# Scores paired by halves, one burst of probability-times-v products a unit, and three score banks a pass, in an adaLN block with segmented attention and a SwiGLU feed-forward

## The chip, the cores and the metric

The kernel runs on one core of a Trainium2 chip. The metric is the device time of one execution in microseconds (us). Before the change three executions took 1886.43, 1879.5 and 1883.25 us, with a median of 1883.25 us.

Engines: PE is the matrix engine (TensorE), PEld its loading of weights, DVE VectorE, ACT ScalarE, POOL GpSimd, and SP the engine that issues most DMAs. PE writes only into PSUM, which has 8 banks of 128 partitions x 512 fp32 numbers; DVE and ACT read the banks.

## The reference, cut to what matters

```python
h = layernorm(x) * (1 + ca) + sa                 # x: 2048 x 576; 32 heads of 18; 4 segments of 512
for s in range(4):                               # per segment and head
    logits = qs @ ks.T * scale + mask            # 512 x 512, causal
    a_dot = softmax(logits) @ vs
    a_mem = phi(qs) @ M / (phi(qs) @ z + 1e-6)   # M, z: from the segments before
    o = g * a_mem + (1 - g) * a_dot
    M += phi(ks).T @ vs;  z += phi(ks).sum()
x = x + ga * (o @ wo)
h = layernorm(x) * (1 + cb) + sb
x = x + gb * ((silu(h @ w_gate) * (h @ w_up)) @ w_down)
```

## The kernel before

There are three stages. Until 237 us, q, k and v are projected (`proj`, `vproj`) and stored in DRAM, for four segments of 512 tokens. From 237 to 592 us runs attention, with the products by `wo` of earlier segments and the preparation of the feed-forward's input mixed in. From 613 us to the end (a short rest of the `wo` products lies between) comes the feed-forward, whose code is the same in both kernels.

Attention works in 32 **units**, of one segment and four heads each (`units`, u = 8 s + q). A head has 18 features, and fp32 accuracy is had by stacking high and low parts, so a score product contracts over 54 or 56 rows. Heads with an even number lie in partitions 0 to 63 of the stacks `kst` and `qst` (half a), odd ones in 64 to 127 (half b). Two score products in different halves of the array can run at once. A score product thus uses PE as two tiles of 64 x 128. A product of exponentials and v uses it as four tiles of 128 x 32, one for each head; all others (`pw`, `px`, `pn`, `pto`, `pt`) use the full 128 x 128.

Each unit has two passes. **Pass 1** (`p1_step`, two units ahead) computes scores to find the row maximum: PE writes them into a bank of tag `s1` (L187), DVE takes the maximum (L206), and `mt_a`/`mt_b` (events m and n) transpose the maxima and put them by DMA into two rows of `qst` for each half. **Pass 2** (`p2_step`) computes the transposed scores less the maximum into a bank `s2` (L639), ACT takes the exponential into a tile `Pt` (L645), and POOL zeroes what the mask forbids (L649). `av_step` multiplies `Pt` with v into the bank `av` (L662) for key blocks j = 0 to 3 of 512, 384, 256 and 128 columns; `ev_step` (E) copies it out by ACT; `comb_a` and `comb_b` (c, d) transpose it back and scale it. `wo_m` and `wo_x` (M0 to M3, X) make a product with `wo` in the bank `pw`, `num_a` to `num_e` (A, B, C, D, G) are the part of the memory, and `trans4` and its successors (at steps from `KP`) prepare the feed-forward.

The order is written by hand. Every unit has eleven steps, and `PAT` (a row for each kind of unit: first or second half of a segment, even or odd) says which events each step issues, in this order on all engines. An event "a" is one call of `scores`: one bank's worth of pass 2 of unit u and one of pass 1 of unit u + 2, 12 calls in a unit. The engines run in order, each its own queue.

PSUM banks before: two `s1`, two `s2`, two `x` (for `px`, `pmt`, `pn`, `pto`, `ptr`, `pt` in turn), one `w` (for `pw`) and one `av`. While `w` has no other work (u < 11) every third bank of pass 1 is the `w` bank, and in units 0 to 3 every third of pass 2 is an `x` bank.

The first two units' pass 1 runs earlier, among the projections of segment 1 (`early`, `p1_unit`). It uses full-height products against `qe`, a copy of q in which the other half is zero.

Of the kernel before, what the change touches and what calls it, by code (L numbers as in the profile page):

```python
# [7 lines left out]
F32 = mybir.dt.float32  # L8
F32R = mybir.dt.float32r
# [6 lines left out]
P = 128  # L16
S = 2048
D = 576
# [4 lines left out]
L = 512  # L23
# [33 lines left out]
NE = 2  # L57
WQ = (0, 3, 4, 5, 6)
E1 = 3
E2 = 2  # L60
PAT = (("a", "a", "M0 a a", "V2 V3 m E D n", "a a", "M1 G c", "Q a a", "V0 M2 d", "a a", "h A0 q M3 R S P X T f a Y B0", "a Z A1 V1 z B1 C"),
# [3 lines left out]
LNA = 1  # L65
S1B, S2B, XB, WB = 2, 2, 2, 1


def f32(ap):
    return ap.bitcast(F32)  # L70
# [3 lines left out]
def block(ctx: ExitStack, tc: tile.TileContext, x, wqk, wv, wo, beta, wgu, wd, c, w_mod, wm01, out):  # L74
    nc = tc.nc
# [81 lines left out]
    turn = [0, 0]  # L157
    HS0 = [[[0, 1, 2, 3]], [[0, 1], [2, 3]]] + [[[0], [1], [2], [3]]] * 2
    HS1 = [[[1], [0], [3], [2]], [[1, 3], [0, 2]]]
    HS2 = [[[0], [1], [2], [3]], [[0, 2], [1, 3]]]  # L160

    def load_stack(u, b):
        s, q = units[u]
        for e in range(2):
            v = [d[s].rearrange("f z t -> (f z) t").rearrange("(Q a e r) t -> Q e r a t", Q=8, a=2, e=2)[q, e]
                 for d in (kD, qD)]
            r = slice(64 * e, 64 * e + 54)
            nc.sync.dma_start(f32(kst[b][r]), v[0])
            nc.sync.dma_start(f32(qst[b][r]), v[1])
            if u < NE:  # L170
                nc.sync.dma_start(f32(qe[u][r, e:4:2, :]), v[1])
# [6 lines left out]
    def p1_step(u, b, i, ps, jp, jb, spare=0, mms=None):  # L178
        if i == 3:
            mcol[u] = (mwk.tile([P, 4, 4], F32, tag="mx", name="mx"),  # L180
                       mwk.tile([P, 2, 2, 2, 4], F32R, tag="mc", name="mc"))
        mx, mc = mcol[u]
        n = 128 * (i + 1)

        def mm(bank, h, o):
            r = slice(64 * (h % 2), 64 * (h % 2) + 54)
            nc.tensor.matmul(bank[:, n * o:n * o + n], lhsT=qst[b][r, h // 2, 128 * i:128 * i + 128],  # L187
                             rhs=kst[b][r, h // 2, 0:n], start=True, stop=True)
        hss = HS1[n <= 256] if mms is not None else HS0[i]
        for hs in hss:  # L190
            turn[0] += 1
            if spare and turn[0] % 3 == 0:
                bank = ps.tile([P, L], F32, tag="w", name="s1", bufs=spare)
            else:
                bank = ps.tile([P, L], F32, tag="s1", name="s1", bufs=S1B)
            if mms is None:
                for o, h in enumerate(hs):
                    nc.tensor.matmul(bank[:, n * o:n * o + n], lhsT=qe[u][0:118, h, 128 * i:128 * i + 128],
                                     rhs=kst[b][0:118, h // 2, 0:n], start=True, stop=True)
            else:  # L200
                for o, h in enumerate(hs):
                    mms.append(lambda h=h, o=o, bank=bank: mm(bank, h, o))
                yield
            for o, h in enumerate(hs):
                junk = jp.tile([P, L], BF16, tag="junk", name="junk", bufs=jb)
                nc.vector.tensor_tensor_reduce(junk[:, :n], bank[:, n * o:n * o + n], tri[:, L - n:],  # L206
                                               1.0, -3e38, op0=ALU.add, op1=ALU.max, accum_out=mx[:, h, i:i + 1])
            if hs is not hss[-1]:
                yield
        if i == 0:  # L210
            mv = mx.rearrange("p (a e) i -> p e a i", e=2)
            nc.gpsimd.tensor_scalar(mc[:, :, 0], mv, -1.0, 0.0, op0=ALU.mult, op1=ALU.add)
# [12 lines left out]
        nc.scalar.copy(mr, pmt.pop(u)[:32, :P])  # L225
        put_m(u, u % NB)

    def p1_unit(u, b, ps, tag, bufs, jp, jb):
        for i in range(4):
            yield from p1_step(u, b, 3 - i, ps, jp, jb)  # L230
        for i in range(6 - 3 * u):
            yield
        mt_a(u, ps, tag, bufs)
        mt_b(u)
# [31 lines left out]
    with ExitStack() as p1:  # L266
# [6 lines left out]
        ps = pool(p1, "ps1", 2, space=PSUM)  # L273

        def early():
            q_ = pb.tile([P, 4, L], F32R, tag="qe", name="qe", bufs=1)
            nc.gpsimd.memset(f32(q_), 0.0)
            qe[0] = qe[1] = q_
            for u in range(NE):
                load_stack(u, u)  # L280
                yield from p1_unit(u, u, ps, "m", 1, pb, 2)
            load_stack(2, 2)

        wqkh = wq1.tile([P, 9, 5, P], F32R, tag="wqkh", name="wqkh")
# [328 lines left out]
    def load_unit(u):  # L613
        if u < NU:
            load_stack(u, u % NB)

    def p1_seq(u, mms):
        if NE <= u < NU:
            for i in range(4):
                yield from p1_step(u, u % NB, 3 - i, ps, wk, 4, WB if u < 11 else 0, mms)  # L620

    Pt, av = {}, {}

    def p2_step(u, j, mms):
        if u >= NU:
            return
        n = L - 128 * j
        pt = pp_.tile([P, 4, n], F32, tag=f"P{j}", name="Pt", bufs=1)
        Pt[u, j] = pt
        for hs in HS2[n <= 256]:  # L630
            turn[1] += 1
            if u < 4 and turn[1] % 3 == 0:
                bank = ps.tile([P, L], F32, tag="x", name="s2", bufs=XB)
            else:
                bank = ps.tile([P, L], F32, tag="s2", name="s2", bufs=S2B)
            for o, g in enumerate(hs):
                def mm(o=o, g=g, bank=bank):
                    r = slice(64 * (g % 2), 64 * (g % 2) + 56)
                    nc.tensor.matmul(bank[:, n * o:n * o + n],  # L639
                                     lhsT=kst[u % NB][r, g // 2, 128 * j:128 * j + 128],  # L640
                                     rhs=qst[u % NB][r, g // 2, 128 * j:L], start=True, stop=True)
                mms.append(mm)
            yield
            per = len(hs)
            nc.scalar.activation(pt[:, hs[0]:hs[-1] + 1:2, :n], bank[:, :n * per].rearrange("p (a b) -> p a b", a=per),  # L645
                                 AF.Exp, scale=SCALE)
            if hs is not HS2[n <= 256][-1]:
                yield
        nc.gpsimd.affine_select(out=pt[:, :, :P], in_=pt[:, :, :P], pattern=[[0, 4], [1, P]], compare_op=ALU.is_ge,  # L649
                                fill=0.0, base=0, channel_multiplier=-1)  # L650
        yield

    def av_step(u, j):
        if u < 0 or u >= NU:
            return
        s, q = units[u]
        if j == 0:
            av[u] = ps.tile([P, L], F32, tag="av", name="av", bufs=1)
        pt = Pt.pop((u, j))
        for h in range(4):  # L660
            hh = 4 * q + h
            nc.tensor.matmul(av[u][32 * h:32 * h + 32, 128 * j:L], lhsT=vq[s][:, j, VW * hh:VW * hh + 32],  # L662
                             rhs=pt[:, h, :L - 128 * j], start=(j == 0), stop=(j == 3))
# [92 lines left out]

    wps = {}

    def wo_m(s, i, h, c, wb=WB):
# [620 lines left out]
    def scores(ga, gb, ma, mb):  # L1380
        next(ga, None)
        next(gb, None)
        while ma or mb:
            for m in (ma, mb):
                if m:
                    m.pop(0)()
        next(ga, None)
        next(gb, None)

    with tc.manual_schedule():  # L1390
        new_stack(3, sk2)
# [56 lines left out]
        for i in range(4):  # L1448
            for h in range(2):
                for c in range(WC):  # L1450
                    n = 8 * i + 4 * h + c
                    wo_m(3, i, h, c, 2)
                    if c == 3:
                        wo_x(3, i, h)
                    flush()
# [232 lines left out]
```

## Time and profile before

| what | us |
|---|---|
| median of three executions | 1883.25 |
| the profiled execution | 1878.65 |
| its span, first to last instruction | 1876.9 |
| attention, first score product to last `px` product | 237.8 to 591.3 |
| PE / DVE / ACT / POOL busy over the span | 1846.5 / 1493.8 / 961.4 / 490.9 |

Busy PE time says little: a matmul is pipelined, the record of one lasts longer than the distance to the next, and a PE that starts its next matmul late still looks busy. What a matmul really costs is read from the distance between the starts of neighbours. An idle time of PEld (weight load) that ended on another engine is a wait that PE's busy time can hide. DVE and ACT records have hardly any overlap, so their busy time is their work.

### The profile page before, as it was taken

How to read it: one execution, taken by the hardware profiler on the slowest of the kernel's cores; microseconds unless marked ns; L12 is line 12 of the kernel's file. 1: busy time of each engine (PE TensorE's matmuls, PEld its weight loads, DVE VectorE, ACT ScalarE, POOL GpSimd, SP SyncE). 2: the span in 40 equal slices, each digit the busy share in tenths (PEclk: the TensorE clock that was granted, in tenths of full speed). 3: DMA queues.
4: the chain of work that ended last, by engine and by line, in shares of the span. 5: the costliest groups of instructions: out<-in, count | busy, mean ns of one | idle time of the engine just before them, and what ended most of it. 6: DMA issues, size and time to landing. Idle time of an engine off the chain costs nothing.

```text
span 1876.9 us, 30994 instructions
## 1 busy us (share of the span) xinstructions
PE 1846.5 (98%) x11061; PEld 1519.5 (81%) x11061; DVE 1493.8 (80%) x3309; ACT 961.4 (51%) x2137; POOL 490.9 (26%) x686
## 2 busy tenths in 40 slices
PE   8999999999999999999999999999999999999999
PEld 5888855666656888888888888888888888888888
DVE  7566378888885888888888889758888888888886
ACT  6344467667776544444544544434454454544442
POOL 2010036454565154454544454300000000000000
PEclk9999999999999999999999999999999999999999
DMA  8677655457655755455545534486333432333331
GB/s 299 220 230 264 230 158 152 139 144 198 172 157 179 272 171 192 164 167 196 176 163 167 163 125 155 149 279 188 107 100 99 126 103 88 114 104 125 103 101 51
DMA packets 177518, 304.49 MB, mean 162 GB/s; under 512 B 25156, under 2 KB 107012, under 8 KB 175444
## 3 DMA queue, kind: packets, MB, share of 16 engines
q1 hardware_dynamic: 149988, 248.66, 42.6%
q10 hardware_dynamic: 27376, 53.86, 8.1%
q8 instruction: 87, 1.43, 0.3%
q14 instruction: 67, 0.55, 0.1%
HBM read 188.42 MB, written 113.33 MB: 161 GB/s over the span
## 4 chain that ended last, share of the span: by engine, by line
PE 89%; DVE 4%; DMA 4%; ACT 2%; issue 1%; POOL 1%; SPq 0%; ACTq 0%; DVEq 0%
PE A L1227 23%; PE pd L1355 13%; PE C L1227 12%; PE pd L1336 10%; PE B L1227 6%; PE pp L100 5%; PE s L639 5%; PE av L662 4%; PE pw L771 3%; PE pv L100 3%; PE s L187 2%; DMA y<-yD 1%; PE pn L828 1%; PE px L683 1%; ACT Pt L645 1%
## 5 line engine op out<-in xcount | busy, mean ns | idle before, releaser
L1227 PE MATMUL A<-y,wh 128*128 128x512 f32 x1152 | 406.1, 393 | 2.0 <-DMA y<-yD 1.0
L206 DVE CUSTOM_DVE_ANT_0 junk<-s,tri 128x256 bf16<-128x256 f32 (+3 forms) x512 | 224.7, 486 | 61.8 <-PE s L187 52.5
L1227 PEld LDWEIGHTS A<-y,wh 128*128 128x128 f32 x1152 | 216.6, 188 | 46.9 <-ACT B L1273 2.2
L1192 DVE TENSOR_TENSOR wl<-O,wh 128x256 fp32r<-128x256 f32 x504 | 245.3, 492 | 2.1 <-ACT wh L1191 1.6
L1227 PE MATMUL A<-y,wl 128*128 128x512 f32 x576 | 226.8, 394 | 0.0
L645 ACT ACTIVATE Pt<-s 128x512 f32<-128x512 f32 (+2 forms) x384 | 183.1, 525 | 79.9 <-PE s L187 61.3
L1341 DVE TENSOR_TENSOR acc<-acc,pd 128x576 f32<-128x576 f32 x216 | 162.2, 751 | 59.0 <-PE pd L1336 51.6
L1227 PE MATMUL C<-y,wh 128*128 128x512 f32 x576 | 203.0, 393 | 0.5 <-DVE cu L1250 0.5
L1191 ACT CAST wh<-O 128x256 fp32r<-128x256 f32 x504 | 197.5, 405 | 1.2 <-DMA yD<-st 1.2
L1365 DVE TENSOR_TENSOR acc<-acc,pd 128x576 f32<-128x576 f32 x156 | 116.9, 750 | 92.2 <-PE pd L1355 91.4
L1355 PE MATMUL pd<-dh,ah 128*128 128x288 f32 x640 | 189.1, 295 | 0.5 <-DVE x L1359 0.5
L1355 PE MATMUL pd<-dh,al 128*128 128x288 f32 x640 | 189.1, 295 | 0.0
L1355 PE MATMUL pd<-dl,ah 128*128 128x288 f32 x640 | 188.8, 295 | 0.0
L1182 POOL TENSOR_TENSOR O<-O 128x384 f32<-128x384 f32 x132 | 149.7, 1147 | 147.3 <-DMA O<-in_wgu_dram 38.3
L1296 ACT CAST ah<-sg 128x512 fp32r<-128x512 f32 x192 | 119.2, 621 | 77.6 <-DVE sg L1251 71.4
L639 PE MATMUL s<-qs,ks 56*128 56x256 f32 (+3 forms) x512 | 141.0, 365 | 6.2 <-ACT Pt L645 5.5
L187 PE MATMUL s<-ks,qs 54*128 54x512 f32 (+1 forms) x480 | 138.9, 374 | 3.8 <-DMA qs<-qD 1.8
L1297 DVE TENSOR_TENSOR al<-sg,ah 128x512 fp32r<-128x512 f32 x192 | 133.6, 696 | 10.7 <-ACT ah L1296 10.5
L1336 PE MATMUL pd<-dh,ah 128*128 128x288 f32 x448 | 133.0, 297 | 0.0
L1336 PE MATMUL pd<-dh,al 128*128 128x288 f32 x448 | 132.5, 296 | 0.0
L1336 PE MATMUL pd<-dl,ah 128*128 128x288 f32 x448 | 132.3, 295 | 0.0
L649 POOL TENSOR_SCALAR_AFFINE_SELECT Pt<-Pt 128x512 f32<-128x512 f32 x128 | 81.5, 637 | 183.5 <-ACT Pt L645 182.9
(372 smaller groups left out, 4382.7 us busy)
## 6 DMA issues: line engine op xcount, KB each, us to landing
O<-in_wgu_dram SPq DMA_DIRECT2D x36, 768.0 KB
O<-oD SPq DMA_DIRECT2D x36, 512.0 KB
oD<-O ACTq DMA_DIRECT2D x34, 512.0 KB
ks<-kD SPq DMA_DIRECT2D x64, 216.0 KB
qs<-qD SPq DMA_DIRECT2D x64, 216.0 KB
O<-in_wgu_dram SPq DMA_DIRECT2D x36, 384.0 KB
rD<-wr ACTq DMA_DIRECT2D x36, 336.0 KB
wr<-rD SPq DMA_DIRECT2D x35, 336.0 KB
```

Of the source, the lines that this page charges most:

```text
L100: nc.tensor.matmul(ps, lhsT=a, rhs=b, start=(k == 0), stop=(k == 13))
L187: nc.tensor.matmul(bank[:, n * o:n * o + n], lhsT=qst[b][r, h // 2, 128 * i:128 * i + 128], rhs=kst[b][r, h // 2, 0:n], start=True, stop=True)
L206: nc.vector.tensor_tensor_reduce(junk[:, :n], bank[:, n * o:n * o + n], tri[:, L - n:], 1.0, -3e38, op0=ALU.add, op1=ALU.max, accum_out=mx ...
L639: nc.tensor.matmul(bank[:, n * o:n * o + n], lhsT=kst[u % NB][r, g // 2, 128 * j:128 * j + 128], rhs=qst[u % NB][r, g // 2, 128 * j:L], st ...
L645: nc.scalar.activation(pt[:, hs[0]:hs[-1] + 1:2, :n], bank[:, :n * per].rearrange("p (a b) -> p a b", a=per), AF.Exp, scale=SCALE)
L1182: eng.tensor_tensor(o[:, d], o[:, a], o[:, b], op=op)
L1191: nc.scalar.copy(wh, o)
L1192: later.append(lambda: nc.vector.tensor_tensor(wl, o, f32(wh), op=ALU.subtract))
L1227: nc.tensor.matmul(bank, lhsT=a, rhs=b, start=(first and n == 0), stop=(n == 6), skip_group_check=not first)
L1336: nc.tensor.matmul(pd[:, i, :288], lhsT=a[:, tk], rhs=w, start=(k == 0), stop=(k == 2))
L1341: nc.vector.tensor_tensor(o, o, pd[:, :, :288], op=ALU.add)
L1355: nc.tensor.matmul(pd[:, i, :288], lhsT=a[:, tk], rhs=w, start=(k == 0), stop=(k == 5))
```

## The change

Five things change, all before 613 us.

1. In `scores` the two lists of matmuls of a call are taken by their half, a first. The calls issue the pairs (a, b), (a, b) where they had issued (a, b), (b, a).
2. The four products of a unit with v stand together in one event, V0123, in the unit after (before: V0 and V1 in the unit itself, V2 and V3 in the one after). `Pt` has two buffers for each j instead of one.
3. Banks: three `s1`, three `s2`, two `x`. `av` and `pw` have no bank of their own any more, and take `x` banks in turn with the others. The spare banks of the first units are gone.
4. `PAT` and `KP` are other tables.
5. The stack of unit 3 is loaded ahead of v at the start of attention. In `early`, `qe` is three tiles of two heads instead of one of four, each unit's pass 1 goes by pairs of heads, and the q stacks of units 0 and 1 are loaded after `early` instead of in it.

```diff
-KP = (7, 8, 1, 3)
+KP = (10, 8, 10, 8)
...
-       ("a a Q", "l M0 a a", "D", "V2 V3 m n M1 E A0 a a", "", "G p M2 B0 a", "a", "M3 X A1 q c x d a a", "f", "B1 V0 C", "V1 Y h a P a"),
+       ("a Q", "a l V0123 E m a n", "", "a a M0 M1", "M2 a a p", "D", "x a a M3 X", "", "q a c a a", "Y P f", "d G"),
...
-S1B, S2B, XB, WB = 2, 2, 2, 1
+S1B, S2B, XB = 3, 3, 2
+PB = (2, 2, 2, 2)
...
-            turn[0] += 1
-            if spare and turn[0] % 3 == 0:
-                bank = ps.tile([P, L], F32, tag="w", name="s1", bufs=spare)
-            else:
-                bank = ps.tile([P, L], F32, tag="s1", name="s1", bufs=S1B)
...
+            bank = ps.tile([P, L], F32, tag="s1", name="s1", bufs=S1B if a is None else 2)
+            for o, h in enumerate(hs):
+                if a is None:
+                    mms.append((h % 2, lambda h=h, o=o, bank=bank: mm(bank, h, o)))
+                else:
+                    nc.tensor.matmul(bank[:, n * o:n * o + n], lhsT=qe[u, a][0:118, h % 2, 128 * i:128 * i + 128],
+                                     rhs=kst[b][0:118, a, 0:n], start=True, stop=True)
...
-            q_ = pb.tile([P, 4, L], F32R, tag="qe", name="qe", bufs=1)
-            nc.gpsimd.memset(f32(q_), 0.0)
-            qe[0] = qe[1] = q_
+            q_ = []
+            for n in range(3):
+                q_.append(pb.tile([P, 2, L], F32R, tag=f"qe{n}", name="qe", bufs=1))
+                nc.gpsimd.memset(f32(q_[n]), 0.0)
...
-        pt = pp_.tile([P, 4, n], F32, tag=f"P{j}", name="Pt", bufs=1)
+        pt = pp_.tile([P, 4, n], F32, tag=f"P{j}", name="Pt", bufs=PB[j])
...
-            turn[1] += 1
-            if u < 4 and turn[1] % 3 == 0:
-                bank = ps.tile([P, L], F32, tag="x", name="s2", bufs=XB)
-            else:
-                bank = ps.tile([P, L], F32, tag="s2", name="s2", bufs=S2B)
+            bank = ps.tile([P, L], F32, tag="s2", name="s2", bufs=S2B)
...
-            av[u] = ps.tile([P, L], F32, tag="av", name="av", bufs=1)
+            av[u] = ps.tile([P, L], F32, tag="x", name="av", bufs=XB)
...
-            wps[0] = ps.tile([P, L], F32, tag="w", name="pw", bufs=wb)
+            wps[0] = ps.tile([P, L], F32, tag="x" if s < 3 else "w", name="pw", bufs=XB if s < 3 else 2)
...
-            j = int(a)
-            av_step(u if j < 2 else u - 1, j)
+            for j in a:
+                av_step(u - 1, int(j))
...
-            for m in (ma, mb):
-                if m:
-                    m.pop(0)()
+            for m in sorted((m for m in (ma, mb) if m), key=lambda m: m[0][0]):
+                m.pop(0)[1]()
...
         new_stack(3, sk2)
+        load_unit(3)
         for j in range(4):
             load_v(0, j)
...
-            load_unit(u + 3)
+            if u:
+                load_unit(u + 3)
```

How the order moves is seen at three places. In the rows, `s` is a score bank of either pass (L639 before and L649 now: pass 2; L187 and L185: pass 1), and numbers at a name's end are buffers.

PE at the start of unit 11 (an odd unit, first half of its segment). Before, from its first score to its first `pw` products:

```order
L639 MATMUL s_4563<-qs_2718,ks_2719 128x512
L187 MATMUL s_4566<-ks_984,qs_983 128x512
L639 MATMUL s_4572<-qs_2718,ks_2719 128x512
L187 MATMUL s_4573<-ks_984,qs_983 128x512
L771 MATMUL pw<-woh,oh 128x288
L771 MATMUL pw<-wol,oh 128x288
L771 MATMUL pw<-woh,ol 128x288
L639 MATMUL s_4590<-qs_2718,ks_2719 128x512
L187 MATMUL s_4591<-ks_984,qs_983 128x512
L639 MATMUL s_4597<-qs_2718,ks_2719 128x512
L187 MATMUL s_4598<-ks_984,qs_983 128x512
L662 MATMUL av<-Pt,vq_3394 32x256 x4
```

Now, from the same score:

```order
L649 MATMUL s_4564<-qs_2728,ks_2729 128x512
L185 MATMUL s_4567<-ks_984,qs_983 128x512
L185 MATMUL s_4574<-ks_984,qs_983 128x512
L649 MATMUL s_4573<-qs_2728,ks_2729 128x512
L672 MATMUL av<-Pt,vq_3423 32x512 x4
L672 MATMUL av<-Pt,vq_3423 32x384 x4
L672 MATMUL av<-Pt,vq_3423 32x256 x4
L672 MATMUL av<-Pt,vq_3423 32x128 x4
L215 MATMUL pmt<-ident,mc 32x128
L649 MATMUL s_4608<-qs_2728,ks_2729 128x512
L185 MATMUL s_4609<-ks_984,qs_983 128x512
```

The four products with v (of unit 10) follow each other, scores stand on both sides of them, and the `pw` products come later in one row of ten. Within a group of four scores, pass 1 comes first in the second pair. Counted over the whole order from the first score of pass 2 to the last `px`, PE changes its tiling 391 times before and 251 times now: score bursts fall from 175 to 124, bursts of products with v from 88 to 32, the others from 153 to 123. Neighbouring scores of the same half fall from 206 to 8. The number of matmuls is the same, 10385.

ACT, exponentials around the copy of `av` in unit 11. Before:

```order
L645 ACTIVATE Pt<-s_4590 128x512
L645 ACTIVATE Pt<-s_4597 128x512
L225 COPY mr<-pmt 32x128
L674 COPY avs<-av 128x512
```

Now, in the same unit:

```order
L655 ACTIVATE Pt<-s_4564 128x512
L655 ACTIVATE Pt<-s_4573 128x512
L684 COPY avs<-av 128x512
L655 ACTIVATE Pt<-s_4608 128x512
L219 COPY mr<-pmt 32x128
```

The copy of `av` had four wide exponentials of its unit ahead of it and now has two, and it stands directly behind the whole burst of products.

SP at the start of attention, around the loads of unit 3's stack (`ks_2719`, `qs_2718` before; `ks_2729`, `qs_2728` now). Before:

```order
L707 DMA vq_2722<-vD_99 128x624 x4
L168 DMA ks_2719<-kD_91 54x2x512
L169 DMA qs_2718<-qD_87 54x2x512
L528 DMA vD_102<-vs_2539 128x2496
L168 DMA ks_2719<-kD_91 54x2x512
L169 DMA qs_2718<-qD_87 54x2x512
```

Now:

```order
L169 DMA ks_2729<-kD_91 54x2x512
L169 DMA qs_2728<-qD_87 54x2x512
L169 DMA ks_2729<-kD_91 54x2x512
L169 DMA qs_2728<-qD_87 54x2x512
L717 DMA vq_2736<-vD_99 128x624
L542 DMA vD_102<-vs_2549 128x2496
L717 DMA vq_2736<-vD_99 128x624 x3
```

All four loads of the stack now stand ahead of the loads of v, and ahead of the store of the last segment's v (`vD_102`), which waits for the end of the projections.

More of the change, by code (lines that the diff above doesn't have):

```diff
@@ L167, in load_stack @@
             r = slice(64 * e, 64 * e + 54)
[L168 to L171, printed above, removed]
+            for n, st in enumerate((kst, qst)):
+                if part & 1 << n:
+                    nc.sync.dma_start(f32(st[b][r]), v[n])
     def put_m(u, b):
@@ L176, in put_m, with p1_step @@
             nc.sync.dma_start(f32(qst[b][64 * e + 54:64 * e + 56]).rearrange("p a t -> p (a t)"), mr[16 * e:16 * e + 16])
-    def p1_step(u, b, i, ps, jp, jb, spare=0, mms=None):
-        if i == 3:
+    def p1_step(u, b, i, ps, jp, jb, mms=None, a=None):
+        if i == 3 and not a:
             mcol[u] = (mwk.tile([P, 4, 4], F32, tag="mx", name="mx"),
@@ L188, in mm @@
                              rhs=kst[b][r, h // 2, 0:n], start=True, stop=True)
[L189 removed]
+        hss = HS1[n <= 256] if a is None else [[2 * a], [2 * a + 1]] if i > 1 else [[2 * a, 2 * a + 1]]
         for hs in hss:
[L191 to L202 removed]
+            bank = ps.tile([P, L], F32, tag="s1", name="s1", bufs=S1B if a is None else 2)
[5 more added lines that the diff above has]
+                                     rhs=kst[b][0:118, a, 0:n], start=True, stop=True)
+            if a is None:
                 yield
@@ L226, in mt_b, with p1_unit @@
         put_m(u, u % NB)
-    def p1_unit(u, b, ps, tag, bufs, jp, jb):
-        for i in range(4):
-            yield from p1_step(u, b, 3 - i, ps, jp, jb)
+    def p1_unit(u, b, ps, tag, bufs, jp, jb, load_e):
+        for a in range(2):
+            for i in range(4):
+                yield from p1_step(u, b, 3 - i, ps, jp, jb, a=a)
+                if (u, a) == (0, 0):
+                    if i == 1:
+                        load_stack(1, 1, 1)
+                        load_e(1, 0)
+                    elif i == 3:
+                        load_e(1, 1)
         for i in range(6 - 3 * u):
@@ L619, in p1_seq @@
             for i in range(4):
-                yield from p1_step(u, u % NB, 3 - i, ps, wk, 4, WB if u < 11 else 0, mms)
+                yield from p1_step(u, u % NB, 3 - i, ps, wk, 4, mms)
     Pt, av = {}, {}
```

30 lines of the change are left out of this document (19 added, 11 removed), and 4 rows, old and new, of the table PAT.

## The prediction

> **What bounds the kernel now.** I read the page first, then the busy time by stretches of the attention stage, the waits of that stage, and PE's timeline of some units.
>
> ```profile
> span 1876.9 us, 30994 instructions
> PE 1846.5 (98%) x11061; PEld 1519.5 (81%) x11061; DVE 1493.8 (80%) x3309; ACT 961.4 (51%) x2137; POOL 490.9 (26%) x686
> PE A L1227 23%; PE pd L1355 13%; PE C L1227 12%; PE pd L1336 10%; PE B L1227 6%; PE pp L100 5%; PE s L639 5%; PE av L662 4%; PE pw L771 3%; PE pv L100 3%; PE s L187 2%; DMA y<-yD 1%; PE pn L828 1%; PE px L683 1%; ACT Pt L645 1%
> ```
>
> PE sets the end nearly everywhere. The feed-forward lines (L1227, L1336, L1355) and the projections (L100) are not touched, so what can change is attention: 237.8 to 591.3 us, 353.5 us for 32 units, 11.0 us a unit.
>
> ```profile
> core 0: us, PE busy (x) PEld busy (x) DVE busy (x) ACT busy (x) POOL busy (x), PEclk, DMA share, GB/s
> 237.80:315.50 77.70, 71.43 (x574) 38.32 (x573) 65.68 (x284) 54.44 (x123) 39.00 (x77) 0.96 0.56 156
> 315.50:434.00 118.50, 116.96 (x945) 71.00 (x943) 98.45 (x409) 78.63 (x171) 56.96 (x125) 1.00 0.52 146
> 434.00:568.70 134.70, 132.23 (x1055) 81.94 (x1055) 115.52 (x468) 97.20 (x217) 72.11 (x144) 1.00 0.63 173
> 568.70:591.30 22.60, 22.25 (x174) 13.13 (x171) 6.47 (x19) 15.55 (x34) 15.19 (x25) 1.00 0.35 110
> ```
>
> In the 30 units up to 568.7 us, DVE works 65.68 + 98.45 + 115.52 = 279.65 of 330.9 us (85%) and ACT 230 (70%). DVE's work doesn't change, so it is the floor: whatever PE saves, these units can't take less than 280 us. The waits tell whether PE's 98% is work:
>
> ```profile
> ACT Pt L645 <- PE s L187: 61.3, 89, 1.8
> DVE junk L206 <- PE s L187: 52.5, 79, 12.4
> PEld s L639 <- ACT Pt L645: 33.5, 87, 1.0
> PEld pw L771 <- issue: 17.0, 59, 0.8
> PEld s L639 <- issue: 16.9, 84, 0.8
> PEld s L187 <- DVE mx L206: 8.9, 28, 0.7
> ```
>
> Both sides wait for each other: PE's weight loads stood 33.5 us on ACT and 8.9 on DVE for a free score bank, while ACT and DVE stood 61 and 52 us for scores. The "issue" rows are of another kind: 0.29 and 0.20 us each time PE goes to another kind of product, with nothing to wait for.
>
> **The change, part by part.** First the price of going from one kind of product to another, by the distance between starts:
>
> ```profile
> 354.02 0.38 PE L639 MATMUL s<-qs,ks 56*128 56x256 f32 x1
> ...
> 354.25 0.28 PE L639 MATMUL s<-qs,ks 56*128 56x256 f32 x1
> ...
> 354.37 0.28 PE L639 MATMUL s<-qs,ks 56*128 56x256 f32 x1
> ...
> 354.49 0.28 PE L639 MATMUL s<-qs,ks 56*128 56x256 f32 x1
> 354.69 1.71 PE L662 MATMUL av<-Pt,vq 128*32 128x512 f32 x16
> 356.33 0.32 PE L639 MATMUL s<-qs,ks 56*128 56x128 f32 x1
> ...
> 359.85 0.86 PE L662 MATMUL av<-Pt,vq 128*32 128x256 f32 x16
> 360.63 0.28 PE L221 MATMUL pmt<-ident,mc 128*32 128x128 f32 x1
> 360.85 0.44 PE L639 MATMUL s<-qs,ks 56*128 56x384 f32 x1
> 360.85 0.61 PE L187 MATMUL s<-ks,qs 54*128 54x384 f32 x2
> 361.13 0.34 PE L639 MATMUL s<-qs,ks 56*128 56x384 f32 x1
> 361.40 0.40 PE L771 MATMUL pw<-woh,oh 128*128 128x288 f32 x1
> 361.63 0.30 PE L771 MATMUL pw<-wol,oh 128*128 128x288 f32 x1
> 361.77 0.29 PE L771 MATMUL pw<-woh,ol 128*128 128x288 f32 x1
> 361.90 0.31 PE L771 MATMUL pw<-woh,oh 128*128 128x288 f32 x1
> 362.04 0.60 PE L683 MATMUL px<-ident,avs 128*128 128x128 f32 x4
> ...
> 363.12 1.07 PE L662 MATMUL av<-Pt,vq 128*32 128x512 f32 x8
> 364.12 0.66 PE L744 MATMUL pto<-ident,o 128*128 128x128 f32 x4
> ...
> 368.60 0.85 PE L662 MATMUL av<-Pt,vq 128*32 128x384 f32 x8
> 369.38 0.50 PE L639 MATMUL s<-qs,ks 56*128 56x512 f32 x1
> ```
>
> - A score burst: four pairs of 256 columns start at 354.02, .25, .37 and .49, and the next product at 354.69. A pair inside costs 0.12, the first 0.11 more, the last 0.08 more. So a burst costs 0.19 beside its pairs. The order has 51 score bursts fewer (175 to 124): 51 x 0.19 = 9.7 us.
> - A burst with v: alone, the blocks take 1.00 (512 columns, 363.12 to 364.12), 0.78 (384, 368.60 to 369.38) and 0.78 (256 and 128, 359.85 to 360.63). Where 512 and 384 stand together they take 1.64 (354.69 to 356.33), not 1.78: 0.14 for each burst saved. 56 fewer (88 to 32): 7.8 us. A whole V0123 is then 2.56 - 2 x 0.14 = 2.28 us.
> - Other bursts: four `pw` products take 0.64 (361.40 to 362.04) at 0.13 each inside, so 0.12 for the burst. 30 fewer (153 to 123): 3.6 us.
>
> Together 21 us of PE time. These are costs of PE alone, and no other engine hides them.
>
> **The third bank of a pass.** The waits for banks are 33.5 + 8.9 = 42.4 us in 115 times. Most begin where PE changes its kind of product, and of each some 0.2 (the issue row: 16.9 us in 84) passes anyway: 42.4 - 115 x 0.2 = 19 us net. Bounds are 0 and 19. Until unit 10 spare banks of `w` and `x` already gave a third, so I take two thirds, 13 us.
>
> **Unit 3's stack.** One wait, in unit 1, goes away with the loads' new place:
>
> ```profile
> L187 PE MATMUL s<-ks,qs 54*128 54x512 f32 (+1 forms) x480 | 138.9, 374 | 3.8 <-DMA qs<-qD 1.8 <-DVE mx L206 1.1 <-DMA pq<-qF 0.4
> ```
>
> That is 1.8 us. The loads of v move back past them, but products with v now begin a unit later.
>
> **Strict alternation of halves.** The four scores of 384 columns at 360.85 were issued a, b, b, a. The first pair starts together, the second 0.28 later, together too (pass 1's two rows are merged), and the burst ends 0.55 after its start: two pairs of 0.18 (0.12 x 384 / 256) and the 0.19. Nothing is lost to the same half, so I take 0.
>
> **What it costs.** The last unit has nothing after its scores to cover its products. Before, its V0 and V1 stood among scores that waited for ACT:
>
> ```profile
> 586.31 1.07 PE L662 MATMUL av<-Pt,vq 128*32 128x512 f32 x8
> 587.72 0.85 PE L662 MATMUL av<-Pt,vq 128*32 128x384 f32 x8
> 590.02 0.58 ACT L674 COPY avs<-av 128x512 f32<-128x512 f32 x1 [1.52 <-PE av L662]
> ```
>
> They move behind the last scores: up to 1.00 + 0.78, so +1.6 us. V3 needs the last exponentials and masks; V0 to V2 (1.00 + 0.64 + 0.43 or so) and two score pairs run ahead of it, about 2.5 us, as much as now. I take 0, and 0.5 a unit (15 us) as the other end. During a V0123 of 2.28 us, ACT and DVE get no scores. Three banks hold three wide tiles for each, at
>
> ```profile
> L206 DVE CUSTOM_DVE_ANT_0 junk<-s,tri 128x512 bf16<-128x512 f32 (+1 forms) x480 | 210.3, 486 | 56.5 <-PE s L187 52.5 <-PE s L639 0.6 <-POOL mc L212 0.3
> L645 ACT ACTIVATE Pt<-s 128x512 f32<-128x512 f32 (+2 forms) x384 | 183.1, 525 | 79.9 <-PE s L187 61.3 <-PE s L639 14.1 <-POOL mc L212 2.1
> ```
>
> 0.5 us each on average, so 1.5 us of cover plus what else DVE has in its queue; DVE starves some 0.7 us a unit. That caps the gain: 279.65 + 30 x 0.7 = 301 us for units 0 to 29, against 330.9, so 30 us. The terms (21 + 13 + 1.8 = 36) exceed the cap, and I take the cap. The early pass 1 has the same matmuls and about the same loads, among projections that keep PE busy: 0, bounds plus and minus 2.
>
> **Sum.** 1878.65 (the profiled execution) - 30 + 1.6 = 1850.3. The median of the runs is 4.6 above that execution; against it, 1883.25 - 28.4 = 1855 us.
>
> **The rivals.** (1) *The consumers are the bound already.* If DVE idles in the new units as it does now (51 us in 30 units, 1.7 each), because a burst of 2.28 us starves it longer than the small bursts did, the saved PE time comes back as bank waits. Only the 1.8 us remain, less the tail's 1.6: about 1883. For it: PE waits on banks already. Against: most of DVE's idle time ended on PE's scores, and PE gets cheaper. The Trainium skill (TensorEngine Tiling (Array Packing), "PSUM Bottleneck") warns that tiling speeds up PE but not the emptying of PSUM; the rows of DVE and ACT here bear out that these are near.
>
> (2) *Slower: `x` becomes the bottleneck.* Two banks must now carry `av` (from V0 until ACT's copy of 0.58) and `pw` (from M0 until X) beside `pmt`, `px`, `pn` and the rest: four to seven tenants a unit where two to five had them. PE is in order, so a late bank stops all behind it, scores too. If two hand-overs a unit come 0.8 us late (a copy and one exponential or reduction ahead of it), that is 32 x 2 x 0.8 = 51 us, against 28 gained: 1883 + 23 = 1906. It decides from 0.45 us a hand-over. For it: ACT's copy stands behind exponentials. Against: between the burst with v and the first `pw` the new order has six scores or more, about 1 us of PE, and in unit 11 two exponentials ahead of the copy instead of four.
>
> (3) *Alternation pays as well.* If a neighbour in the same half exposes its weight load, the 0.11 us of a burst's start, 198 fewer of them are worth 22 us, and DVE doesn't cap it: 1855 - 22 = 1833. Against: the burst at 360.85. The Trainium skill (TensorE: Matmul & The Clock Gate, "Part 3: Packing small matmuls", "The mechanism") says that a weight load overlaps a running matmul only when the row group differs, which would make this the outcome; that burst doesn't agree.
>
> **Chances.** My forecast 0.57; (3) 0.07; (1) 0.17; (2) 0.19. A measurement of this kernel tells about 0.5% (9.4 us) from no change. Forecast and (3) count as faster, with some of (1): 0.68. Same 0.14, slower 0.18. The likeliest case's own range is 1840 to 1868 (cap at 0.3 or 1.1 us of DVE idle a unit, and the bounds of the early part). The 8-in-10 range takes in (1) and the edge of (2) and (3): 1836 to 1888.
>
> **What would show it.** After: attention near 325 us; bursts with v at 2.3 us; the PEld waits on ACT for `s` under 15 us; DVE busy over 90% in units 0 to 29; no wait on `qs` in unit 1; four scores of 384 columns still 0.55. Wrong, if PEld waits of `pw`, `pn` or `av` on ACT or DVE add up to over 20 us (2), or DVE's idle time on scores stays near 50 us (1).

## The result, and the profile after

| | median, us | lowest to highest |
|---|---|---|
| before | 1884.84 | 1879.5 to 1886.72 |
| the change | 1861.76 | 1859.87 to 1864.9 |

The ratio of the times is 0.9884, 95% interval 0.9857 to 0.9911: faster by 23.1 us, where 28.4 were forecast. The two profiled executions differ by less, 1878.65 - 1864.9 = 13.75 us, because they lie on opposite sides of their medians (6.2 below, 3.1 above). A second pair, shown last among the experiments, differs by 16.24 us. Neither pair holds the whole 23.1, so where the remaining 7 to 9 us lie isn't shown.

The first lines of the profile's page of the changed kernel, with busy time by engine and the chain of waits:

```profile
span 1863.2 us, 31096 instructions
PE 1824.8 (98%) x11061; PEld 1521.6 (82%) x11061; DVE 1493.3 (80%) x3309; ACT 957.9 (51%) x2137; POOL 494.5 (27%) x688
PE A L1237 24%; PE pd L1365 13%; PE C L1237 12%; PE pd L1346 10%; PE B L1237 6%; PE pp L101 5%; PE av L672 4%; PE pv L101 3%; PE pw L781 3%; PE s L185 2%; PE s L649 2%; DVE junk L200 2%; DMA qs<-mr 1%; DMA y<-yD 1%; PE pn L838 1%
```

PE's busy time falls by 21.7 us and DVE's stays (1493.8 to 1493.3). In the chain, pass 2's scores shrink from 5% to 2%. Two entries are new: DVE's row maximum (`junk`) and the DMA of the maxima into the stacks (`qs<-mr`).

Where the time went is read by stretches that begin at the same work: unit 0's first pass-2 score, unit 9's and unit 30's. The columns are those of the prediction's view of stretches. Before:

```profile
237.80:325.00 87.20, 80.37 (x649) 42.89 (x648) 74.64 (x319) 62.25 (x140) 45.90 (x91) 0.96 0.56 157
325.00:568.70 243.70, 240.25 (x1921) 148.37 (x1917) 205.01 (x840) 168.01 (x370) 122.18 (x255) 1.00 0.58 160
```

After, the same units:

```profile
238.80:332.50 93.70, 83.42 (x634) 46.95 (x633) 73.31 (x314) 61.55 (x139) 46.42 (x90) 0.87 0.51 151
332.50:557.20 224.70, 216.39 (x1919) 145.76 (x1915) 198.25 (x835) 163.52 (x367) 119.65 (x251) 1.00 0.59 170
```

Units 9 to 29 are 19.0 us shorter, 0.90 a unit; DVE works 88% of the stretch where it had worked 84%. Units 0 to 8 are 6.5 us *longer*. The start of attention is 1.0 later, and attention as a whole, to its last `px` product, takes 342.2 us where it took 353.5. From unit 30 on nothing is lost: the first product of the feed-forward (`A`) starts 44.3 us later before (613.0 - 568.7) and 42.7 us later after (599.9 - 557.2).

Some of the waits of units 0 to 29 after the change (engine, what waited, what ended the wait: us in total, times, longest):

```profile
DVE junk L200 <- PE s L185: 29.4, 20, 12.3
ACT avs L684 <- PE av L672: 24.6, 15, 3.9
ACT Pt L655 <- PE s L185: 22.0, 33, 1.6
ACT mr L219 <- PE pmt L215: 21.4, 14, 3.3
DVE junk L200 <- PE s L649: 20.6, 25, 3.3
PEld s L185 <- DVE mx L200: 17.2, 54, 1.3
ACT Pt L655 <- PE s L649: 12.0, 26, 1.5
PEld s L649 <- ACT Pt L655: 9.2, 26, 0.8
```

Pass 2's wait for a bank fell from 33.5 us in 87 times to 9.2 in 26, and ACT's for scores of pass 1 from 61.3 to 22.0. Pass 1's wait for a bank rose, from 8.9 to 17.2. (The rows of before, in the prediction, hold the last two units too.) ACT's waits moved more than they fell: it now waits 24.6 us for a burst with v (`av`) and 21.4 for the `pmt` behind it, where it waited 7.5 and 3.6 in the same units. DVE's waits for scores of either pass come to 50.0 us, where they were 53.1; by stretches they went from 31.8 to 19.3 in units 9 to 29 and from 21.3 to 30.7 in units 0 to 8.

### The profile page after: what moved, and what is told of

The parts are those of the page before. It is cut to its first block, busy times and chain, and to the rows that moved or that the text cites. A ratio compares the mean times of both kernels' runs of the same rounds, so it can differ in the third digit from the quotient of the medians.

```text
span 1863.2 us, 31096 instructions
## 1 busy us (share of the span) xinstructions
PE 1824.8 (98%) x11061; PEld 1521.6 (82%) x11061; DVE 1493.3 (80%) x3309; ACT 957.9 (51%) x2137; POOL 494.5 (27%) x688
## 4 chain that ended last, share of the span: by engine, by line
PE 89%; DVE 5%; DMA 3%; ACT 1%; issue 1%; POOL 1%; SPq 0%; ACTq 0%; DVEq 0%; POOLq 0%
PE A L1237 24%; PE pd L1365 13%; PE C L1237 12%; PE pd L1346 10%; PE B L1237 6%; PE pp L101 5%; PE av L672 4%; PE pv L101 3%; PE pw L781 3%; PE s L185 2%; PE s L649 2%; DVE junk L200 2%; DMA qs<-mr 1%; DMA y<-yD 1%; PE pn L838 1%
## 5 line engine op out<-in xcount | busy, mean ns | idle before, releaser
L200 DVE CUSTOM_DVE_ANT_0 junk<-s,tri 128x384 bf16<-128x384 f32 (+3 forms) x512 | 221.1, 485 | 53.1 <-PE s L185 29.4
L1202 DVE TENSOR_TENSOR wl<-O,wh 128x256 fp32r<-128x256 f32 x504 | 244.8, 491 | 2.1 <-ACT wh L1201 1.6
L655 ACT ACTIVATE Pt<-s 128x512 f32<-128x512 f32 (+2 forms) x384 | 178.9, 525 | 37.0 <-PE s L185 22.0
L1307 DVE TENSOR_TENSOR al<-sg,ah 128x512 fp32r<-128x512 f32 x192 | 136.7, 712 | 10.2 <-ACT ah L1306 10.0
L649 PE MATMUL s<-qs,ks 56*128 56x256 f32 (+3 forms) x512 | 127.9, 362 | 6.3 <-ACT Pt L655 3.5
L185 PE MATMUL s<-ks,qs 54*128 54x512 f32 (+1 forms) x480 | 127.0, 367 | 4.7 <-DVE mx L200 3.7
L1365 PEld LDWEIGHTS pd<-dh,ah 128*128 128x128 f32 x640 | 120.8, 189 | 6.8 <-DVE x L1369 0.8
```

The costliest lines, as they stand in the source:

```text
L649: nc.tensor.matmul(bank[:, n * o:n * o + n], lhsT=kst[u % NB][r, g // 2, 128 * j:128 * j + 128], rhs=qst[u % NB][r, g // 2, 128 * j:L], st ...
L1202: later.append(lambda: nc.vector.tensor_tensor(wl, o, f32(wh), op=ALU.subtract))
L1365: nc.tensor.matmul(pd[:, i, :288], lhsT=a[:, tk], rhs=w, start=(k == 0), stop=(k == 5))
```

## The experiments

All start from the changed kernel; ratios are against the kernel before, with 95% intervals. Units 0 to 8 and 9 to 29 are those of the stretches above; "half" is the time at a granted clock of 0.5 in units 0 to 29, summed from the clock's records.

| kernel | median, us | ratio | units 0-8, us | units 9-29, us | half, us |
|---|---|---|---|---|---|
| before | 1884.84 | 1 | 87.2 | 243.7 | 6.8 |
| the change | 1861.76 | 0.9884 | 93.7 | 224.7 | 23.9 |
| halves not sorted | 1863.78 | 0.9898 | 93.7 | 225.1 | 23.9 |
| burst in two parts | 1866.88 | 0.9914 | 88.6 | 231.2 | 13.7 |
| banks 2, 2, 2 | 1971.78 | 1.0468 | 117.5 | 299.5 | 102.4 |
| banks 3, 2, 3 | 1926.36 | 1.0221 | 110.8 | 263.4 | 68.3 |
| banks 2, 3, 3 | 1960.02 | 1.0403 | 123.7 | 290.1 | 102.4 |
| maxima's DMA by ACT | 1903.18 | 1.0109 | 106.1 | 250.0 | 68.3 |
| a product to fill | 1867.34 | 0.9916 | 94.7 | 227.1 | 17.1 |
| maxima's DMA amid the loads | 1889.41 | 1.003 | 106.6 | 238.2 | 54.6 |
| unit 3's stack late | 1867.37 | 0.9925 | 97.4 | 224.7 | 30.7 |
| two parts until unit 8 | 1860.3 | 0.9885 | 90.6 | 224.7 | 17.1 |

### Halves not sorted

```diff
-            for m in sorted((m for m in (ma, mb) if m), key=lambda m: m[0][0]):
+            for m in [m for m in (ma, mb) if m]:
```

> The change, with the scores of a call issued as before (pass 2, then pass 1; a b b a). If alternation is worth nothing, as forecast: within 3 us of the change (0.988 of before). If a neighbour in the same half exposes 0.11 us of weight load, 198 neighbours come back: 22 us slower than the change, about 1.000 of before.

0.9898 (0.9877 to 0.9918) against 0.9884 (0.9857 to 0.9911): the intervals overlap, and neither stretch differs by more than 0.4 us. The alternation is worth nothing that can be measured here. A group of four scores of 384 columns in the changed kernel, on PE's timeline (start, us, instruction):

```profile
348.62 0.44 PE L649 MATMUL s<-qs,ks 56*128 56x384 f32 x1
348.62 0.61 PE L185 MATMUL s<-ks,qs 54*128 54x384 f32 x2
348.90 0.33 PE L649 MATMUL s<-qs,ks 56*128 56x384 f32 x1
```

The second pair starts 0.28 after the first, as it did in the order a, b, b, a. The Trainium skill's rule (TensorE: Matmul & The Clock Gate, "Part 3: Packing small matmuls", "The mechanism"), by which a weight load overlaps only another row group, would have made a difference; the trace doesn't agree.

### The burst with v in two parts

```diff
-       ("a Q", "a l V0123 E m a n", "", ...
+       ("a Q", "a l V01 m a n V23 E", "", ...
```

The other three rows of `PAT` are split in the same way, with one event `a` (a bank of scores of each pass) between the parts, and the copy of `av` (E) behind the second.

> The change, with the burst of products with v cut in two (V01, then scores, then V23): 32 bursts with v and about 32 bursts of scores more. If bursts cost what the trace of before shows (0.14 and 0.19 us): 10.6 us slower than the change, 0.994 of before. If the long burst starves DVE and ACT, and that costs as much as it saves: no slower than the change.

```profile
238.50:327.10 88.60, 79.39 (x633) 44.14 (x633) 72.76 (x314) 62.10 (x139) 46.39 (x90) 0.92 0.56 161
327.10:558.40 231.30, 221.90 (x1920) 141.84 (x1918) 197.90 (x836) 165.80 (x367) 119.78 (x251) 1.00 0.58 165
```

Units 9 to 29 take 6.6 us more, 0.31 for each of the 21 units. The prediction's price for one burst with v and one score burst more, which is what the order of these units now holds, is 0.14 + 0.19 = 0.33. That is the direct test of these two terms, net of what shorter bursts spare DVE and ACT, and they hold: in five profiles with the burst whole these units lie between 224.7 and 225.1 us. Units 0 to 8 gain 5.1 us instead, with less half clock, so the whole kernel is 5.1 us slower by the medians, not the 10.6 forecast.

### Two banks for a pass again, three ways

```diff
-S1B, S2B, XB = 3, 3, 2
+S1B, S2B, XB = 2, 2, 2
```

The two other kernels have 3, 2, 3 and 2, 3, 3. The first leaves two banks of PSUM unused.

> The change, with two score banks a pass instead of three (two PSUM banks stay unused). If the third bank was worth 13 us, as forecast: 10 to 16 us slower than the change, 0.994 to 0.996 of before, and PE's weight loads wait 30 us or more on ACT for s again. If DVE's own pace bounds the units: within 3 us of the change.

> The change, with the third bank of pass 2 (s2) given to x: s1 three, s2 two, x three. Two banks each made it 110 us slower than the change. If that was pass 2's missing bank (ACT): 50 to 110 us slower than the change. If it was pass 1's (DVE): within 10 us. If x, shared by av and pw, held the change back, its third bank would show here as a gain against what the missing s2 bank costs.

> The change, with the third bank of pass 1 (s1) given to x: s1 two, s2 three, x three. If pass 1's bank (DVE) is what counts: 50 to 110 us slower than the change; if pass 2's: within 10 us.

All three are slower than the kernel before. The waits of units 0 to 29, first with 2, 2, 2:

```profile
PEld s L185 <- DVE mx L200: 63.7, 101, 1.9
PEld s L649 <- ACT Pt L655: 40.3, 72, 1.6
```

With 3, 2, 3:

```profile
PEld s L649 <- ACT Pt L655: 76.5, 137, 1.6
```

With 2, 3, 3:

```profile
PEld s L185 <- DVE mx L200: 102.3, 148, 1.9
```

Wherever a pass has two banks, PE waits for that pass's reader, and the other pass stands too: with 3, 2, 3 DVE waits 49.1 us for scores of pass 1, where it waits 29.4 in the change. Both passes need the third bank, and a third `x` bank doesn't make up for a missing one. The three banks are therefore no term of 13 us beside the others: the new order costs 65 (3, 2, 3) to 110 us (2, 2, 2) more without them, the lower clock that comes with it included. The old order, with two banks and its spare ones, waited 42.4 us for banks in all; that smaller bursts are what made two enough is argued, since that order wasn't run with other banks, nor the new order with the old layout, where `av` and `pw` have banks of their own.

### The DMA of the row maxima by ACT

In the changed kernel PE waits twice for the maxima at the start of units 6 and 8. SP's and PE's timelines:

```profile
290.52 0.29 SPq L169 DMA_DIRECT2D ks<-kD  x1
...
291.64 0.34 SPq L169 DMA_DIRECT2D qs<-qD  x1
292.33 0.63 SPq L174 DMA_DIRECT2D qs<-mr  x1
...
299.20 0.59 PE L649 MATMUL s<-qs,ks 56*128 56x512 f32 x1 [1.06 <-DMA qs<-mr]
...
321.64 0.47 PE L649 MATMUL s<-qs,ks 56*128 56x512 f32 x1 [1.51 <-DMA qs<-mr]
```

The four loads of a stack (the first and the last are shown) are issued just ahead of the small DMA. In the chain of waits (start, us, what) it takes almost 7 us each time:

```profile
292.33 6.74 DMA qs<-mr
314.52 6.98 DMA qs<-mr
```

So I gave it another queue.

```diff
-            nc.sync.dma_start(f32(qst[b][64 * e + 54:64 * e + 56]).rearrange("p a t -> p (a t)"), mr[16 * e:16 * e + 16])
+            (nc.scalar if u >= NE else nc.sync).dma_start(f32(qst[b][64 * e + 54:64 * e + 56]).rearrange("p a t -> p (a t)"), mr[16 * e:16 * e + 16])
```

> The change, with the two small DMAs of the row maxima issued by ACT instead of SP, so that they don't stand behind the four stack loads in SP's queue. If those loads make the rows late (the chain shows 6.74 and 6.98 us from issue to use in units 5 and 7, PE waiting 1.06 and 1.51): these waits go, the clock doesn't fall behind them, and the kernel is 3 to 8 us faster than the change (0.984 to 0.987 of before). If all queues share the same engines and only the transfers' volume counts: no change.

Slower by 41 us than the change. The rows of that line, with the shortest, median and longest duration in ns:

```profile
L174 ACTq DMA_DIRECT2D qs<-mr x60: 618/621/1287, 253.6 to 600.9; - x60
  ACT Pt L655: 9.6, 7
  ACT avs L684: 8.1, 6
```

Each issue holds ACT's queue for 0.62 us, two in a unit; exponentials and the copy of `av` stand behind them, and PE's wait for a bank of pass 2, which ACT frees, rises from 9.2 to 36.7 us. So ACT had no 1.2 us a unit to spare. PE's two waits for the maxima (2.6 us) are gone, as forecast, but the half clock didn't fall, it rose from 23.9 to 68.3 us. Whether the waits went because of the queue stays open, since a slower stretch leaves the DMA more time.

### The same DMA amid the loads

```diff
+                if u < NU - 3:
+                    load_stack(u + 3, (u + 3) % NB, 2)
...
-                load_unit(u + 3)
+                load_stack(u + 3, (u + 3) % NB, 1)
```

The k half of a stack is loaded at the unit's start as before, the q half only behind the DMA of the maxima.

> The change, with a unit's two loads of q stacks issued behind the DMAs of the row maxima instead of ahead of them (the k stacks stay at the unit's start). Issued by ACT instead, these DMAs cost ACT 1.28 us a unit, and the run told nothing of the queue. If the loads ahead make the maxima late in units 5 and 7: the waits of 1.06 and 1.51 us go, fewer windows of half clock follow, and the kernel is 2 to 6 us faster than the change. If the q stacks then come late for pass 1 of the next unit: slower.

28 us slower than the change: 12.9 us in units 0 to 8 and 13.5 in 9 to 29. PE's timeline shows what may be late, in unit 11:

```profile
360.62 0.59 PE L185 MATMUL s<-ks,qs 54*128 54x512 f32 x2 [1.19 <-DVE r L702]
```

The wait is put down to a DVE instruction whose result this product doesn't read; the last reduction that DVE made of a score bank had ended at 359.92. This is the first product with a new stack, whose q half was issued at 355.51, 5.1 us ahead. That the load is what is late is argued from this, not shown. Here too PE no longer waits for the maxima, and the half clock rose all the same, to 54.6 us. So taking the two waits away didn't take the half clock away.

### Unit 3's stack late again

```diff
-        load_unit(3)
...
-            if u:
-                load_unit(u + 3)
+            load_unit(u + 3)
```

> The change, with unit 3's stack loaded behind v again, as before. If its new place is worth the wait it took away: 1 to 3 us slower than the change, with a wait of 1.8 us or more on qs in unit 1. If products with v, now a unit later, or other work cover it: no different.

```profile
PE s L185 <- DMA qs<-qD: 3.0, 1, 3.0
```

The wait on `qs` is back, and units 0 to 8 take 97.4 us, 3.7 more, with 6.8 us more of half clock. The forecast had 1.8 for this step. Units 9 to 29 don't change. By the medians the kernel is 5.6 us slower, more than the 1 to 3 forecast, though the intervals still touch (0.9906 to 0.9945, and 0.9857 to 0.9911).

### A product to fill, and the split burst in the first units only

In units 0 to 8, PE is granted half the clock for some stretches. To see whether more work on PE would hold the clock, a product that nobody reads was added to each of these units:

```diff
+                if k == 10 and u < 9:
+                    fl = ps.tile([P, L], F32, tag="x", name="fl", bufs=XB)
+                    nc.tensor.matmul(fl, lhsT=ident, rhs=tri, start=True, stop=True)
```

> The change, with one more product of 128x512 fp32 numbers (0.85 us, into an x bank that nobody reads) at the end of each of units 0 to 8. If half clock in these units is what eats the gain there, since PE falls idle (23.8 us at clock 0.5 in the profile): the half-clock time falls below 10 us, and the kernel is 2 to 8 us faster than the change. If units 0 to 8 are slow for other reasons: 0 to 10 us slower, by the products' own 9 x 1.1 us where they aren't hidden.

Half clock in units 0 to 8 fell from 23.9 to 13.7 us, but the nine products cost some 1.0 us each themselves, and the stretch took 94.7 us. The last experiment shows 20.5 us of half clock there without any edit, so this one decides little.

The split burst was better in units 0 to 8 and worse after, so both were joined:

```diff
-                for ev in PAT[q // 4 * 2 + u % 2][k].split():
+                for ev in (PAT0 if u < 9 else PAT)[q // 4 * 2 + u % 2][k].split():
```

> The change, with the burst cut in two (as in the split run) only in units 0 to 8. The split run took units 0 to 8 in 88.6 us against the change's 93.6, with 13.7 us at half clock against 23.9, and units 9 to 29 in 231.2 against 224.8. If the two stretches don't depend on each other: units 0 to 8 near 89, 9 to 29 near 225, 5 us faster than the change (0.985 to 0.987 of before). If the gain in the first units was chance of the profiled execution: no different from the change.

0.9885 (0.986 to 0.991): not to be told from the change. Units 0 to 8 took 90.6 us, but for the changed kernel that number moves from one execution to the next, as follows.

### Both kernels profiled once more

The mean granted clock of the profiled execution before was 0.998, while the median over the timed executions of that kernel is 0.994, as it is for the change. So the first pair of profiles may not be a fair one.

> The kernel before, unchanged, for a second profiled execution. Two theories of why units 0 to 8 took 87.2 us before and 93.6 after in the two profiled executions, with 6.8 and 23.9 us at half clock. (A) The change brings the half clock: then this execution is like the first, units 0 to 8 at 86 to 89 us, at most 10 us at half clock, mean clock 0.997 or more. (B) The half clock wanders from execution to execution of either kernel, and the first profiled execution of before had unusually little (its mean clock was 0.998, the median of its timed executions 0.994): then mean clock 0.992 to 0.996, 15 to 30 us at half clock, and units 0 to 8 at 90 to 96 us. Units 9 to 29 stay at 243 to 246 us by both.

> The changed kernel, unchanged, for a second profiled execution. By (A) units 0 to 8 take 92 to 95 us again with 20 us or more at half clock; by (B) the half clock in units 0 to 8 may be anything from 10 to 25 us, and the time there 87 to 94 us, moving by half to one us for each us of it. Units 9 to 29 at 224 to 226 us by both.

Before, in its second profile (1880.46 us):

```profile
238.10:327.30 89.20, 84.34 (x649) 44.74 (x648) 74.62 (x319) 62.37 (x140) 45.94 (x91) 0.90 0.54 154
327.30:570.90 243.60, 240.24 (x1919) 148.35 (x1915) 205.00 (x840) 168.02 (x370) 122.19 (x255) 1.00 0.57 160
```

The change, in its second (1864.22 us):

```profile
238.70:329.90 91.20, 81.27 (x633) 46.44 (x633) 73.37 (x314) 61.43 (x139) 46.52 (x90) 0.89 0.53 155
329.90:554.90 225.00, 216.56 (x1920) 145.83 (x1918) 198.40 (x836) 163.60 (x367) 119.81 (x251) 1.00 0.59 170
```

Units 9 to 29 repeat within 0.3 us: 18.6 shorter here, 19.0 in the first pair. Units 0 to 8 don't: the half clock there was 17.1 us before and 20.5 after, and the stretch is 2.0 us longer now, not 6.5. So 4.5 us of the first pair's loss belonged to those two executions. For the kernel before this is theory (B), with its 89.2 us just under the 90 to 96 named. For the change neither is shown alone: 91.2 us lies in (B)'s range, but four windows of half clock came back at the same places (from 244.8, 255.0, 268.7 and 299.4 us first, from 244.4, 254.6, 268.2 and 299.0 now), as (A) has it, and only the fifth, at 323.3, is gone. By the second pair the stretch gains nothing, where 9 us were forecast.

## Why the prediction was right, and where it wasn't

**Bursts (21 us, capped at 30 with the rest).** Right, for units 9 to 29, where no half clock disturbs either kernel: the order has 31 score bursts, 36 bursts with v and 22 others fewer there, 13.6 us by the prediction's prices, and the split burst gave two of these prices together as 0.31 for 0.33. The stretch gained 19.0 us, 0.90 a unit, where the cap gave 1.0. The other 5.4 us weren't separated; PE's weight loads wait 21.9 us for score banks in these units before and 11.6 after. A whole V0123 takes 2.3 us at full clock, as worked out, in each of these 21 units and in three of the units before, of which this is one:

```profile
279.90 2.36 PE L672 MATMUL av<-Pt,vq 128*32 128x512 f32 x32
282.20 0.28 PE L215 MATMUL pmt<-ident,mc 128*32 128x128 f32 x1
```

**The third bank (13 us).** This term is mis-sized, and its form is wrong: it was added to the bursts, but in no layout tried were the bursts had without it. It was priced by the waits of the old order, while its job is to cover those of the new one, where it is worth 65 to 110 us.

**The cap (30 us).** It was right in direction for units 9 to 29, and wrong in both of its numbers. Its floor is DVE's busy time, taken for DVE's work because records were said to have hardly any overlap. They do overlap: reductions that wait for nothing follow each other in 0.34 us, while each record lasts 0.42. Before:

```profile
344.13 0.42 DVE L206 CUSTOM_DVE_ANT_0 junk<-s,tri 128x256 bf16<-128x256 f32 x1
344.47 0.42 DVE L206 CUSTOM_DVE_ANT_0 junk<-s,tri 128x256 bf16<-128x256 f32 x1
```

All DVE records of units 0 to 29 add up to 352.6 us before, in 279.6 us of busy time. After, 348.7 us of records (a few instructions now run later) take 271.6. The busy time shrinks where the work stands closer, so 280 us was no floor. And DVE's idle time, forecast at 0.7 us a unit with 0.3 and 1.1 as its bounds, fell only from (243.7 - 205.0) / 21 = 1.84 to (224.7 - 198.25) / 21 = 1.26 us in units 9 to 29, and rose in units 0 to 8. DVE is busy 85% of units 0 to 29, not over 90% as named, and attention takes 342.2 us, not near 325. Pass 2's wait for ACT, 9.2 us, is under the 15 named. What bounds units 9 to 29 now wasn't tested.

**Units 0 to 8.** Here the step that failed is "30 units" in the cap: it gave these nine units 9 us of gain like the others. They gained nothing. The chain of waits of this stretch, by line, before:

```profile
by line: PE s L639 24.9%; PE av L662 19.5%; DMA qs<-qD 10.2%; ACT Pt L645 8.5%; PE s L187 6.2%; PE px L683 6.0%; PE pn L828 5.7%; DMA qs<-mr 4.9%; DVE junk L206 2.4%; issue 2.2%; PE pmt L221 1.9%; ACT woh L933 1.5%; ACT avs L674 0.8%; ACT n
```

After the change:

```profile
by line: PE av L672 27.1%; DMA qs<-mr 14.6%; PE s L185 14.5%; DVE junk L200 12.1%; PE s L649 9.2%; issue 4.2%; POOL woraw L941 3.0%; ACT Pt L655 2.8%; PE px L693 1.7%; PE pn L838 1.7%; PE pmt L215 1.5%; POOL Pt L659 1.4%; ACT mr L219 1.2%; 
```

The load of a stack (10.2%) is gone as forecast, but the DMA of the row maxima goes from 4.9 to 14.6%, and DVE's maximum from 2.4 to 12.1%: the way from pass 1 through DVE and the DMA to pass 2 is now over a quarter of the chain. The second profile has about the same shares (14.9 and 10.0%). The chain also holds every burst with v (27.1%), and here lies a good part of the missing gain. At full clock the eight bursts would take 2.29 us each to the next product's start, as they do later; five of them, in windows of half clock, take 3.16 to 4.42, which is 7.0 us more in all (5.3 us, on four bursts, in the second profile). These units also have fewer products with `wo`, and until unit 10 the old kernel had spare banks: the prediction takes that off the bank term (19 to 13), but the cap that it uses instead of the sum gives them a full share. The order saves bursts worth 5.7 us here by the prediction's prices, and none of it is seen. How the rest divides between the way of the maxima, the banks and the clock isn't settled: the two attempts at the DMA made other things late.

**The loads' new place (1.8 us).** Right in kind: putting the loads back brought a wait of 3.0 us. The size is uncertain, since the wait was 1.8 us in the first profile before and 0.2 in the second, and the 3.7 us that the units lost hold more half clock too.

**Strict alternation (0), the tail (+1.6), V3 (0), the early part (0 ± 2).** The first is shown. The tail's cost isn't seen in the net: from unit 30 on the time is 1.6 us shorter. In units 9 to 29 no burst with v is held up once it has begun; in the last unit PE waits 1.23 us for a mask, ahead of V2 and not of V3. The early part moved attention by 1.0 us in one pair and 0.6 in the other; its edits weren't undone alone.

**The rivals.** (1), the consumers as the bound already, named as its sign that DVE's idle time on scores stays near 50 us. Over units 0 to 29 it does (53.1 and 50.0). It falls for units 9 to 29, with 19 us gained and that idle time down from 31.8 to 19.3; for units 0 to 8 its outcome came, no gain and more idle time, but there the bursts at half clock lengthen the starving. (2), the `x` banks, falls by the sign that it named, waits of over 20 us. In units 0 to 29 the waits that it means come to 10.2; these are the largest:

```profile
PEld pn L838 <- ACT nm L847: 2.7, 4, 0.7
PEld pn L838 <- DVE xr L786: 2.6, 4, 1.0
PEld pw L781 <- ACT avs L684: 1.9, 6, 0.3
```

A third `x` bank beside three of each pass can't be had in eight, so what it would be worth there wasn't tried. (3) falls with the unsorted halves.

The forecast of 1855 us is 7 below the median. In the profiles the shortfall lies in units 0 to 8 (9 us of gain forecast, 2 to 6.5 lost); units 9 to 29 gave 19 of their 21 us, and the tail came out 3 better. That the total came as near as 23.1 for 28.4 is in part luck: the cap's two numbers were off, and the timed executions show more gain than either pair of profiles.

## What to carry to other kernels

Count how often PE changes its kind of product, price one change by the distance between starts, and check that each reader has banks enough to sit through the longest burst: here the bursts and the banks were one change, not two terms. Add up an engine's records beside its busy time before calling that time a floor. Price a saving stage by stage: here nine units gave nothing, though the order saved bursts there too. Before explaining a difference of a few microseconds between two profiles, look at the granted clock of both against that of the other executions.

## What the hardware showed that I had not expected

**The granted clock drops in a stage that is far from idle.** Four stretches of the changed kernel's first profile, in pairs, and two of the one before:

```profile
265.30:268.70 3.40, 2.26 (x22) 1.67 (x22) 3.33 (x18) 2.29 (x7) 1.27 (x2) 1.00 0.35 112
268.70:272.10 3.40, 3.40 (x15) 1.01 (x19) 1.96 (x12) 1.18 (x3) 1.26 (x4) 0.50 0.59 183
...
319.90:323.30 3.40, 1.89 (x12) 0.89 (x14) 2.58 (x14) 1.88 (x6) 3.02 (x8) 1.00 0.60 160
323.30:326.70 3.40, 3.40 (x32) 1.28 (x24) 1.39 (x5) 0.55 (x2) 1.56 (x3) 0.50 0.55 164
```

```profile
246.50:250.00 3.50, 1.67 (x11) 0.98 (x15) 1.26 (x5) 1.61 (x4) 1.55 (x5) 1.00 0.66 177
250.00:256.80 6.80, 6.80 (x45) 3.73 (x49) 5.20 (x24) 4.62 (x11) 1.95 (x4) 0.50 0.48 145
```

PE was busy for 1.7 to 2.3 of 3.4 us, and the next 3.4 or 6.8 us ran at half the clock. Two other such stretches followed busier ones, so this isn't the whole rule. A burst with v that falls into one takes up to twice as long:

```profile
247.00 4.50 PE L672 MATMUL av<-Pt,vq 128*32 128x512 f32 x32
```

The Trainium skill (TensorE: Matmul & The Clock Gate, "HAM oscillation — how this bites in real kernels") tells of this for a PE that waits for DMA and puts the loss at half of the time so spent. Here the pairs of executions lie on both sides of that: 10.3 us more of it went with 2.0 us in the kernel before, and 3.4 us less of it with 2.5 us in the change, one execution against one.

**A missing bank comes with a lower clock.** With banks 2, 2, 2 the half clock rose to 102 us, against 24 in the change. It comes with the waits for banks; what each is worth alone wasn't separated.
